# Attention and a mixture of experts on one core: early feed-forward blocks in fp16 for two resident experts, with weights loaded once and split in place

## The chip, the core and the metric

The kernel runs on one core of a Trainium2 chip. The metric is the device time of one execution in microseconds. A core has these engines: PE (TensorE, the matrix array, with PEld its weight loads), DVE (VectorE), ACT (ScalarE), POOL (GpSimd) and SP (SyncE, which issues most DMAs here). Each works through its own queue in order; semaphores tie them together.

## What is computed

Two layers follow each other. First an attention with a window of 128 keys and a bias that falls with distance, for 8 batches x 8 heads x 576 positions x 64 dimensions; then a mixture of 8 experts over the 4608 tokens of width 512, in which each token goes to its two best experts.

```python
# attention, per batch and head
scores = scale * q @ k.T + bias, where 0 <= row - column < 128, else -1e9
x = softmax(scores) @ v                                  # 4608 x 512 in all
# experts
noisy = x @ w_gate + log1p(exp(x @ w_noise)) * noise      # 4608 x 8
top2  = the two largest of noisy; g = softmax over the two
out[token] += g * (relu(x[token] @ w1[e]) @ w2[e])        # for both experts e; w1: 512 x 1024, w2: 1024 x 512
```

## The kernel before, in words

The program is written by a planner. Each piece of work is a small generator ("strand") that yields operations with an engine, an estimated duration and a rank; `Order.run` simulates the engines with these estimates and always issues the waiting operation of lowest rank. The result is a fixed order in each engine's queue. Where an operation may run on two engines (`either`, or an `Op` with two entries), the simulated engine that is free first takes it; constants such as `LATE` shift the rank for the second engine.

**Attention.** 32 pairs of heads (four to a batch) go through scores on PE (L455, L448), bias and row maximum on DVE (L473), exponentials on ACT (L480), transposes on PE (L492), their copies `pT` on ACT or DVE (L245, L249), and the product with the values on PE (L523). All in fp32. Per batch, `row_major` scales and stores x to DRAM (`xs`), and `gate` makes logits: a matmul (L655), a transpose, a product (L671) and a sum over the heads on DVE (L676).

**Routing.** When a batch's logits are there, `route(b)` picks the two best experts, counts ranks with matmuls, and builds each expert's list of tokens: a table of lines (`which_line`, one DVE instruction of 128x800, L759), a table of places (`which_place`, ten DVE instructions of 128x64, L765), and ten matmuls of the two (L770). The list is added to a table in DRAM by a GpSimd scatter (L843). Route b+1 waits for route b's scatter.

**Experts, early part.** After two batches (`CUTS = (2,)`), the first 256 list entries of experts 0 to 3 are computed while attention goes on: four blocks in fp32r. Each operand is split into a high and a low part, and three products (high x high, low x high, high x low) are summed. Weights come in eight chunks per expert, of w1 128x4x128 and of w2 128x512; a chunk is loaded to `raw1`/`raw2`, its high part is a copy on ACT or DVE, its low part a subtraction on GpSimd or DVE (L962). A block has 96 matmuls of 256 columns (L1086) and 48 of 512 (L1136).

**Experts, late part.** When all routes are sent (`second_wave`), the rest follows in fp16 with the same three products: experts 0 to 3 have blocks of 512 and 448 rows, experts 4 to 7 of 512, 384 and 320 rows. All weights are loaded a second time. fp16 needs a scale by a power of two: for expert 0 the weights' maximum is taken from the early chunks (L966), for the others from a load of their own (`mraw`, eight of 512 KB, L987, L988). Then `scaled_weight` makes the high part (ACT or DVE) and the low part (DVE, L1023). Gathered tokens get a scale each (`fit`: L1051, L440, L441, L1047 to L1049, and a copy), are transposed (L1066) and split (L1076). After the first product comes relu, with its high part on ACT or DVE (L1108, L1110) and its low part on DVE (L1125). The last block of an expert forms its second product transposed (L1141), and its rows are turned back (L1196). Results are scaled and added to the output by GpSimd scatters (L1215). A loop at the end treats experts with over 1216 tokens.

## Time and profile before

| | |
|---|---|
| time, median of 3 runs | 1222.68 us (1221.63 to 1223.39) |
| span of the profiled execution, first to last instruction | 1217.5 us |
| instructions | 20871 |
| last matmul of attention ends (L523) | 328.3 us |
| last list product (L770) | 393.3 us |
| last early block ends (L1136) | 413.8 us |
| first late matmul (L1086) | 428.6 us |
| last matmul | 1204.7 us |
| mean granted clock of PE | 0.988 |

The times in the lower part are counted from the span's start. A row of the profile's groups reads: line, engine, operation, written tile <- read tiles, shape, count | busy us, mean ns of one | idle us of the engine just ahead of them, and what ended it. A row of the timeline has start, duration, engine, line, operation and count. A row of the stretches has the stretch, its length, and for each engine the busy time and number of instructions, then the granted clock, the DMA share and GB/s. A row of one line's instructions has the shortest, median and longest in ns.

### The profile page before, as it was taken

What the parts mean: (1) busy time and instruction counts of PE and PEld (TensorE: products, weight loads), DVE (VectorE), ACT (ScalarE), POOL (GpSimd) and SP (SyncE); (2) the same over time, 40 slices, a digit from 0 to 9 for tenths busy, and PEclk for the clock granted to TensorE, in tenths of its full rate; (3) what the DMA queues carried; (4) which work ended last, traced back from release to release, by engine and by line L of the source; (5) the groups of instructions that cost most, each with busy time, mean ns of one, the idle gap of its engine ahead of it and who ended that gap; (6) DMA issues with size and microseconds to landing.
All of it is one profiled execution on the core that took longest, in us unless ns stands there. A gap on an engine that the chain in (4) does not pass through costs nothing.

```text
span 1217.5 us, 20871 instructions
## 1 busy us (share of the span) xinstructions
PE 1141.3 (94%) x7356; PEld 685.2 (56%) x7356; DVE 765.7 (63%) x2493; ACT 542.2 (45%) x1362; POOL 292.5 (24%) x332
## 2 busy tenths in 40 slices
PE   6998999989987699999999999999999999999995
PEld 4666676667766444545545545445745664575552
DVE  7799887888888893574565646643763473363310
ACT  8777766667633542433424424422632341253211
POOL 5000111241245502033123213302223320322211
PEclk9999999999999889999999999999999999999998
DMA  8896544453266773564655636613763282342221
GB/s 287 303 306 224 162 146 148 142 163 107 67 186 162 191 250 71 181 190 73 192 144 110 186 112 157 187 57 61 206 176 61 54 271 58 62 113 45 35 26 23
DMA packets 133626, 173.35 MB, mean 142 GB/s; under 512 B 25489, under 2 KB 85137, under 8 KB 133521
## 3 DMA queue, kind: packets, MB, share of 16 engines
q1 hardware_dynamic: 115600, 131.68, 34.0%
q0 software_dynamic: 17920, 40.33, 17.5%
q8 instruction: 59, 0.97, 0.3%
q14 instruction: 47, 0.38, 0.1%
HBM read 130.57 MB, written 41.40 MB: 141 GB/s over the span
## 4 chain that ended last, share of the span: by engine, by line
PE 73%; DVE 15%; DMA 7%; issue 2%; ACT 2%; POOL 1%; SPq 0%; another core or an unknown queue 0%; POOLq 0%; DVEq 0%; ACTq 0%
PE bank L1086 26%; PE bank L1136 19%; PE bank L1141 8%; PE bank L523 5%; PE bank L492 4%; PE bank L455 4%; DMA mraw<-in_w_dram 4%; DVE wam L988 3%; PE bank L1066 2%; DMA raw<-in_w_dram 2%; DVE p L473 1%; PE bank L632 1%; DVE hot L765 1%; DMA xg<-xs_dram,ix 1%; PE bank L655 1%
## 5 line engine op out<-in xcount | busy, mean ns | idle before, releaser
L1125 DVE SCALAR_TENSOR_TENSOR bhl<-bank,bhh 128x512 f16<-128x512 f32 (+3 forms) x160 | 97.3, 608 | 300.5 <-ACT bhh L1108 300.4
L1215 POOL DMA_INDIRECT out_dram<-yo,ix x72 | 113.7, 1580 | 560.6 <-ACT yo L245 452.9
L1108 ACT ACTIVATE bhh<-bank 128x512 f16<-128x512 f32 (+3 forms) x150 | 80.4, 536 | 354.5 <-PE bank L1086 353.5
L1086 PE MATMUL bank<-bxh,w1hb 128*128 128x512 f16 (+3 forms) x640 | 223.0, 348 | 0.7 <-ACT bxh L245 0.7
L1086 PE MATMUL bank<-bxl,w1hb 128*128 128x512 f16 (+3 forms) x640 | 222.9, 348 | 0.1
L1086 PE MATMUL bank<-bxh,w1lb 128*128 128x512 f16 (+3 forms) x640 | 222.9, 348 | 0.0
L1086 PEld LDWEIGHTS <-w1hb 128*128 128x128 f16 x1280 | 124.8, 98 | 107.8 <-issue 4.3
L1136 PE MATMUL bank<-w2hb,bhl 128*128 128x512 f16 (+1 forms) x376 | 142.6, 379 | 4.4 <-DVE bhl L1125 4.4
L1136 PE MATMUL bank<-w2hb,bhh 128*128 128x512 f16 (+1 forms) x376 | 142.8, 380 | 0.5 <-ACT bhh L1108 0.5
L1136 PE MATMUL bank<-w2lb,bhh 128*128 128x512 f16 (+1 forms) x376 | 142.5, 379 | 0.0
L480 ACT ACTIVATE p<-p,nm 128x256 f32<-128x256 f32 (+2 forms) x288 | 133.7, 469 | 13.3 <-DVE nm L473 13.2
L1136 PEld LDWEIGHTS <-bhh 128*128 128x128 f16 (+1 forms) x752 | 72.0, 98 | 78.2 <-issue 4.6
L473 DVE CUSTOM_DVE_ANT_0 p<-bank,bias 128x256 f32<-128x256 f32 (+2 forms) x288 | 95.5, 380 | 15.2 <-PE bank L455 11.8
L1086 PEld LDWEIGHTS <-w1lb 128*128 128x128 f16 x640 | 62.8, 98 | 55.9 <-issue 1.2
L523 PE MATMUL bank<-pT,vraw 128*64 128x128 f32 (+3 forms) x896 | 81.0, 303 | 5.3 <-ACT p L480 2.7
L492 PE MATMUL bank<-ident,p 128*128 128x128 f32 x512 | 83.2, 285 | 1.8 <-ACT p L480 0.5
L1034 POOL DMA_INDIRECT xg<-xs_dram,ix x72 | 71.5, 993 | 50.5 <-ACT bxh L245 25.4
L988 DVE TENSOR_REDUCE wam<-mraw 128x1 f32<-128x1024 f32 x56 | 67.4, 1210 | 18.1 <-DMA mraw<-in_w_dram 18.1
L455 PE MATMUL bank<-qk 64*128 64x256 f32 (+1 forms) x512 | 69.9, 383 | 8.8 <-DMA qk<-in_qk_dram 4.7
L962 POOL TENSOR_TENSOR w1la<-raw,w1ha 128x512 fp32r<-128x512 f32 x28 | 38.3, 1367 | 156.2 <-ACT w1ha L245 94.6
L1141 PE MATMUL bank<-bhl,w2hb 128*128 128x448 f16 (+1 forms) x224 | 73.8, 330 | 0.0
L1141 PE MATMUL bank<-bhh,w2hb 128*128 128x448 f16 (+1 forms) x224 | 73.8, 330 | 0.0
(219 smaller groups left out, 2007.6 us busy)
## 6 DMA issues: line engine op xcount, KB each, us to landing
raw<-in_w_dram SPq DMA_DIRECT2D x192, 256.0 KB, 3.6
mraw<-in_w_dram SPq DMA_DIRECT2D x56, 512.0 KB, 6.7
qk<-in_qk_dram SPq DMA_DIRECT2D x32, 608.0 KB, 4.3
out_dram<-xg SPq DMA_DIRECT2D x10, 1024.0 KB, 8.3
vraw<-in_v_dram SPq DMA_DIRECT2D x16, 512.0 KB, 4.5
xs_dram<-x SPq DMA_DIRECT2D x32, 256.0 KB, 4.0
vraw<-in_v_dram SPq DMA_DIRECT2D x16, 128.0 KB, 4.9
xg<-xs_dram,ix POOLq DMA_INDIRECT x72, 4.9
```

The lines of the kernel that those rows point to most:

```text
L455: nc.tensor.matmul(s[h][:, o:o + c], qk[half, i * 128:i * 128 + 128], qk[half, QW + k0:QW + k0 + c], start=True, stop=True)
L473: nc.vector.tensor_tensor_reduce(out=p[:, z, h, 0:c], in0=s[h][:, o:o + c], in1=bv, scale=-0.125, scalar=3.0e38, op0=OP.add, op1=OP.min, a ...
L480: nc.scalar.activation(pv, pv, AF.Exp, bias=nm[:, z, h:h + 1], scale=-1.0, accum_out=den[:, z, 2 * g + h:2 * g + h + 1])
L492: nc.tensor.transpose(t[:, z], p[:, h, a:a + 128], ident)
L523: nc.tensor.matmul(o[half, o0:o0 + c], t[p0:128, kb, hh:hh + D], w, start=m == 0, stop=m == len(lst) - 1)
L988: yield dve(1.13, rank, lambda: nc.vector.tensor_reduce(o, t, axis=AX.X, op=OP.max, apply_absolute_value=True))
L1086: nc.tensor.matmul(t[:, 0:blk.n], wp[:, c], x[:, c, 0:blk.n], start=c == 0 and z == 0, stop=c == 3 and z == 2)
L1108: nc.scalar.activation(o, i, AF.Relu)
L1125: yield dve(0.07 + c * 0.00104, rank - MIDDLE, lambda: nc.vector.scalar_tensor_tensor(hl[:, 0:c], t[:, 0:c], 0.0, high, op0=OP.max, op1=OP ...
L1136: nc.tensor.matmul(blk.y[j][0:r], h[:, cs], wp, start=f == 0 and m == 0, stop=f == 7 and m == 2)
L1141: nc.tensor.matmul(blk.y[c][:, 0:blk.n], wp[:, c * 128:c * 128 + 128], h[:, 0:blk.n], start=f == 0 and m == 0, stop=f == 7 and m == 2)
L1215: ins = nc.gpsimd.indirect_dma_start(out=out, out_offset=bass.IndirectOffsetOnAxis(ap=blk.ix[0:r, j:j + 1], axis=0), in_=t[0:r], in_offset ...
```

## The change

- **Early blocks.** `CUTS = (2, 4, 6)`: after two, four and six batches, 256 more list entries of experts 0 and 1 alone are computed: six blocks, in fp16 with `fit`, in the sequence (0,0), (0,1), (1,0), (1,1), (0,2), (1,2) of expert and cut. The late blocks of experts 0 and 1 shrink to one of 448 rows; experts 2 to 7 have 512, 384 and 320.
- **Weights.** Each weight is loaded once. A held tile of 128x1024 fp32 takes a chunk of w1 and w2; there are 16, and 8 more from the second wave on, with 2 spares. The maximum is taken from the loaded chunk (the loads of `mraw` go). The split writes the four fp16 parts into a spare tile; when both halves are split, the raw tile is the next spare. The tiles of experts 0 and 1 stay until their late block is done; an expert's tiles go back when its last block has used them.
- **GpSimd.** The low parts of experts 0 and 1 may run on GpSimd as two instructions (scale, subtract). For all batches but the last, the head sums of the logits run on GpSimd in three additions, and the two tables are made in narrow compares (four for each of five row groups) on GpSimd or DVE.
- Durations, ranks and thresholds of the planner have new numbers, so all orders move. Of this table:

```diff
-CUTS = (2,)
-FIRST = (256,)
-NF = 4
+CUTS = (2, 4, 6)
+EARLY, STEP = 2, 256
-BLOCKS = (((256, 512), (768, 448)), ((0, 512), (512, 384), (896, 320)))
+BLOCKS = (((768, 448),), ((0, 512), (512, 384), (896, 320)))
+HELD, MORE = 16, 8
+SEQUENCE = ((0, 0), (0, 1), (1, 0), (1, 1), (0, 2), (1, 2))
```

The logits and the tables:

```diff
-        yield dve(0.36 if nz == 1 else 0.5, rank, lambda: nc.vector.tensor_reduce(
-            lgs[b % 2][0:rows, i:i + nz], lt[0:rows, 0:nz].rearrange("p z h e -> p z e h"), axis=AX.X, op=OP.add))
+            G.tensor_add(lv[:, :, 0:4], lv[:, :, 0:4], lv[:, :, 4:8])
+            G.tensor_add(lv[:, :, 0:2], lv[:, :, 0:2], lv[:, :, 2:4])
+            G.tensor_add(lgs[b % 2][0:rows, i:i + nz], lv[:, :, 0], lv[:, :, 1])
...
+        def tables(eng, i):
+            for k in range(2):
+                eng.tensor_scalar(hot[0][:, 2 * i + k], steps_, ef[:, i, k:k + 1], None, op0=OP.is_equal)
+            which_place(eng, i)
...
-        yield dve(0.98, rank, which_line)
-        for i in range(NQ):
-            yield dve(0.28, rank, lambda: which_place(i))
+        if b == B - 1:
+            yield dve(0.98, rank, which_line)
+            for i in range(NQ):
+                yield dve(0.41, rank, lambda: which_place(nc.vector, i))
+        else:
+            for i in range(NQ):
+                yield Op((("POOL", 1.36, rank), ("DVE", 0.86, rank + LATE[10])), lambda g: tables(engine[g], i))
```

The weights:

```diff
+    def weight(e, f, z, t, src, rank):
         yield from move(2.6e5, rank, lambda: nc.sync.dma_start(t, src))
-        yield either(0.52, 0.34, rank, LATE[5], lambda g: copy(g, hi, t))
-        yield Op((("POOL", 1.23, rank), ("DVE", 0.6, rank + WEIGHTS_LATE)),
-                 lambda g: engine[g].tensor_sub(lo, t, hi.bitcast(F32)))
+        yield dve(0.6, rank + (BIG if e >= EARLY else 0), lambda: nc.vector.tensor_reduce(
+            wam[:, e % 2, z, f:f + 1], t, axis=AX.XY if z == 0 else AX.X, op=OP.max, apply_absolute_value=True))
+        mark(seen[e])
+
+    def parts_of_weights(e):
+        yield seen[e]
+        yield from powers_of_weights(e, early_rank(e, 0) + (BIG if e >= EARLY else 0))
+        for f in range(8):
+            rank = early_rank(e, f) + (PARTS if e >= EARLY else 0)
+            t = yield (spares, rank)
+            chunks[e, f] = [Event(), Event(), halves_of(t), t]
...
+                spawn(split(e, f, z, raws(held_[e, f])[z], halves_of(t)[2 * z:2 * z + 2], rank, both))
+            spawn(turn_over(both, held_[e, f]))
...
+    def split(e, f, z, t, parts, rank, both):
...
+        yield either(0.52, 0.6, rank, LATE[5], lambda g: copy(g, hi, t, scale=sc))
+        def low(g):
+            if g == "POOL":
+                nc.gpsimd.tensor_scalar(t, t, sc, None, op0=OP.mult)
+                nc.gpsimd.tensor_sub(lo, t, hi)
+            else:
+                nc.vector.scalar_tensor_tensor(lo, t, sc, hi, op0=OP.mult, op1=OP.subtract)
+        if e < EARLY:
+            yield Op((("POOL", 2.3, rank), ("DVE", 0.66, rank + WEIGHTS_LATE)), low)
+        else:
+            yield dve(0.66, rank, lambda: low("DVE"))
```

Order on DVE and GpSimd, where the tables of the third batch are made (`ef` holds the line and `d` the place of each row, `hot` the two tables). DVE before:

```order
L759 TENSOR_TENSOR hot_167<-ef,steps 128x800
L473 ISA p_86,nm_90<-bank_66,bias_127 128x192
L473 ISA nm_90 128x1
L765 TENSOR_SCALAR hot_168<-steps,d,numbers 128x64 x2
L249 COPY xu_94<-bank_70 128x256
L765 TENSOR_SCALAR hot_168<-steps,d,numbers 128x64 x2
```

GpSimd now, ahead of the scatter of the same list:

```order
L777 TENSOR_SCALAR hot_179<-steps,ef 128x80 x2
L783 TENSOR_SCALAR hot_180<-steps,d,numbers 128x64 x2
L777 TENSOR_SCALAR hot_179<-steps,ef 128x80 x2
L783 TENSOR_SCALAR hot_180<-steps,d,numbers 128x64 x2
L864 MEMSET pad 1x1
L865 DMA slots_dram<-listed,line_of_158 704x64
L682 TENSOR_TENSOR lt_111<-lt_111 128x2x64
```

The tables have left DVE's queue, where attention's maxima stood between them, and stand one behind the other in GpSimd's, with the next batch's logit sums behind the scatter.

Order on PE, where the last early block meets the first late one (`ahh`, `ahl` are the early blocks' parts behind relu, `bxh`, `bxl` the late blocks' tokens). Before:

```order
L1136 MATMUL bank_70<-w2ha_180,ahh_212 128x512
L1136 MATMUL bank_70<-w2la_181,ahh_212 128x512
L1136 MATMUL bank_70<-w2ha_180,ahl_214 128x512
L1066 MATMUL bank_69<-ident,xg_121 128x128 x4
L1066 MATMUL bank_69<-ident,xg_122 128x128 x4
L1066 MATMUL bank_69<-ident,xg_123 128x128 x4
L1066 MATMUL bank_69<-ident,xg_124 128x128 x4
L1086 LDWEIGHTS w1hb_4531
L1086 MATMUL bank_66<-bxh_4521,w1hb_4531 128x512
```

Now:

```order
L1145 MATMUL bank_73<-held_128,ahh_211 128x512
L1145 LDWEIGHTS ahl_214
L1145 MATMUL bank_73<-held_128,ahl_214 128x512
L1097 LDWEIGHTS spare_131
L1097 MATMUL bank_66<-bxh_4602,spare_131 128x448
L1097 LDWEIGHTS spare_131
L1097 MATMUL bank_66<-bxl_4604,spare_131 128x448
```

The transposes of the late tokens no longer stand between the two parts; they stand ahead, among early matmuls. In PE's order the last matmul of attention now has 4.31 of six early blocks behind it (2.38 of four before), and the last list product three of six (about 0.7 of four before).

More of the change, by code (lines that the diff above doesn't have):

```diff
@@ L276, in attention_moe @@
     zero = zeros[:, 0:DM]
-    scratch = [z.rearrange("p a b -> p (a b)") for z in raw1.free]
+    scratch = spares.free
     relc, m1 = scratch[0][:, 0:256], scratch[0][:, 256:512]
@@ L361, in columns @@
             nc.vector.tensor_copy(line_of[0], first_line)
-            nc.vector.tensor_scalar(least[:, 0], iota8, float(NF), float(FIRST[0]), op0=OP.is_lt, op1=OP.mult)
+            for z in range(len(CUTS)):
+                nc.vector.tensor_scalar(least[:, z], iota8, float(EARLY), float(STEP * (z + 1)), op0=OP.is_lt, op1=OP.mult)
         yield pool(0.4, 2, small)
@@ L900, in block_rings @@
                 "hh": ring(pool_, hn, [128, c], dt, name + "hh"), "hl": ring(pool_, hn, [128, c], dt, name + "hl")}
-    wsets = [Ring([weight_set(keep, F32R, f"a{z}") for z in range(5)]), Ring([])]
     wam = keep.tile([128, 2, 2, 8], F32, name="wam")
@@ L907, in attention_moe @@
     back = keep.tile([128, E], F32, name="back")
-    seen = {(e, f): Event(2) for e in range(EARLY) for f in range(8)}
+    seen = [Event(16) for _ in range(E)]
     sized = [Event() for _ in range(E)]
@@ L911, in attention_moe @@
     yor = ring(keep, 2, [128, DM], F32, "yo")
-    rings1 = block_rings(keep, FIRST[0], F32R, "a", 2)
+    rings1 = block_rings(keep, STEP, F16, "a", 3)
     ixr, ytr = Ring([]), Ring([])
-    first = [Block(e, 0, FIRST[0], CUTS[0] * S, rings1) for e in range(NF)]
+    first = [Block(e, STEP * z, STEP, CUTS[z] * S, rings1) for e, z in SEQUENCE]
+    for blk, (_, z) in zip(first, SEQUENCE):
+        blk.cut = z
     second, lists2 = [], []
-    fitr = Ring([])
+    fitr = ring(keep, 4, [128, 3], F32, "fit")
     chunks = {}
@@ L1009, in powers_of_weights @@
         mark(sized[e])
-    def all_powers():
-        for e in range(EARLY):
-            for f in range(8):
-                yield seen[e, f]
-            yield from powers_of_weights(e, ranks1[8 * e + 7] + SIZES[0])
-    def scaled_weight(t, r, hi, lo, ev, rank, src, e, z, f):
-        yield from move(2.6e5, rank, lambda: nc.sync.dma_start(t, src))
-        yield sized[e]
-        sc = wsc[:, e, z:z + 1].bitcast(F32)
-        yield either(0.52, 0.6, rank, LATE[5], lambda g: copy(g, hi, t, scale=sc))
-        yield dve(0.6, rank, lambda: nc.vector.scalar_tensor_tensor(lo, t, sc, hi, op0=OP.mult, op1=OP.subtract))
-        put(r, t)
-        mark(ev)
     def tokens(blk, rank):
@@ L1057, in turn_tokens @@
         yield order.now + 2.3
-        if blk in second:
-            yield from fit(blk, j, r, xg, rank)
+        yield from fit(blk, j, r, xg, rank)
         a = yield (tb, rank)
@@ L1100, in ups @@
                 yield (own, rank)
-            us = 3 * (blk.n / 2400 + (0.005 if p else 0.016))
-            for c in range(4):
-                end = yield pe(us, rank, lambda: mm1(blk, t, ev[2], (c,)), False)
+            us = 3 * (blk.n / 2400 + 0.005)
+            for cc in ((0, 1, 2, 3),) if blk.cut is not None else ((0,), (1,), (2,), (3,)):
+                end = yield pe(us * len(cc) + (0.1 if blk.cut is not None else 0.0), rank,
+                               lambda: mm1(blk, t, ev[2], cc), False)
             spawn(middle(blk, f, t, rank, end))
@@ L1123, in middle @@
             e, hh[:, 0:c], t[:, 0:c]))
[L1124 removed]
         yield dve(0.07 + c * 0.00104, rank - MIDDLE, lambda: nc.vector.scalar_tensor_tensor(
[L1126 removed]
+            hl[:, 0:c], t[:, 0:c], 0.0, hh[:, 0:c], op0=OP.max, op1=OP.subtract))
         put(hbr, t)
@@ L1175, in after @@
         if w:
-            if p == 0 and blk.e < EARLY:
-                yield seen[blk.e, f]
-            put(wsets[p], w)
+            put(held, w)
     def flipped(blk, c, rank, end):
@@ L1255, in second_wave @@
         rings2 = block_rings(more, 512, F16, "b", 3)
-        for z in range(10):
-            put(wsets[1], weight_set(more, F16, f"b{z}"))
+        for z in range(HELD, HELD + MORE):
+            put(held, more.tile([128, 2 * DM], F32, name=f"held{z}"))
         for z in range(2, 3):
@@ L1263, in second_wave @@
         for z in range(4):
-            put(fitr, more.tile([128, 3], F32, name=f"fit{z}"))
-        for z in range(4):
             put(ixr, more.tile([128, 4], I32, name=f"ix{z}"))
-        spawn(size_of_weights(ring(more, 3, [128, 1024], F32, "mraw")))
         t = yield (tb, 0)
         put(yb, t)
-        second.extend(Block(e, s0, c, NPAD, rings2) for e in range(E) for s0, c in BLOCKS[e >= NF])
+        second.extend(Block(e, s0, c, NPAD, rings2) for e in range(E) for s0, c in BLOCKS[e >= EARLY])
         for blk, after_ in zip(second, second[1:] + [None]):
```

215 lines of the change are left out of this document (100 added, 115 removed).

## The prediction

> **What bounds the kernel now.** I read the page's head first, then the busy time of each engine in three stretches: up to the last matmul of attention, from there to the first matmul of the late feed-forward blocks, and the late blocks themselves.
>
> ```profile
> span 1217.5 us, 20871 instructions
> PE 1141.3 (94%) x7356; PEld 685.2 (56%) x7356; DVE 765.7 (63%) x2493; ACT 542.2 (45%) x1362; POOL 292.5 (24%) x332
> ...
> core 0: us, PE busy (x) PEld busy (x) DVE busy (x) ACT busy (x) POOL busy (x), PEclk, DMA share, GB/s
> 0.00:328.10 328.10, 303.89 (x2724) 218.42 (x2724) 273.74 (x1245) 230.74 (x815) 59.94 (x75) 1.00 0.59 189
> 328.10:428.60 100.50, 75.92 (x523) 61.86 (x522) 87.65 (x260) 40.53 (x85) 52.03 (x49) 0.92 0.66 177
> 428.60:1204.70 776.10, 761.45 (x4113) 404.92 (x4112) 404.31 (x991) 270.23 (x462) 176.26 (x204) 1.00 0.47 120
> ```
>
> The late stretch is PE alone: 761 of 776 us busy, every other engine near half. There, only fewer columns save time. In the first two stretches DVE is busy for 83% and 87%, and PE's busy time overstates it, since a matmul's record outlives the start of the next. The starts show the true rate:
>
> ```profile
> 371.06 0.28 PE L1086 MATMUL bank<-axh,w1ha 128*128 128x256 f32 x1
> 371.18 0.28 PE L1086 MATMUL bank<-axl,w1ha 128*128 128x256 f32 x1
> ...
> 373.57 0.40 PE L1136 MATMUL bank<-w2ha,ahh 128*128 128x512 f32 x1
> 373.80 0.40 PE L1136 MATMUL bank<-w2la,ahh 128*128 128x512 f32 x1
> ...
> 1000.08 0.38 PE L1136 MATMUL bank<-w2hb,bhh 128*128 128x512 f16 x1
> 1000.29 0.38 PE L1136 MATMUL bank<-w2lb,bhh 128*128 128x512 f16 x1
> ```
>
> An early fp32r matmul of 256 columns starts 0.12 us after the one ahead, one of 512 columns 0.23 us; an fp16 one of 512 takes 0.215 us. An early block has 96 matmuls of 256 columns and 48 of 512, so 11.5 + 11.0 = 22.5 us of PE in fp32r.
>
> **Term 1, the late blocks: about -46 us.** Their first matmuls are these (the L523 row is the end of attention):
>
> ```profile
> 327.69 0.60 PE L523 MATMUL bank<-pT,vraw 128*64 128x64 f32 x8
> ...
> 428.61 0.58 PE L1086 MATMUL bank<-bxh,w1hb 128*128 128x512 f16 x1 [0.69 <-ACT bxh L245]
> ...
> 473.17 0.35 PE L1086 MATMUL bank<-bxh,w1hb 128*128 128x448 f16 x1
> ...
> 512.32 0.38 PE L1086 MATMUL bank<-bxh,w1hb 128*128 128x512 f16 x1
> ...
> 770.39 0.38 PE L1086 MATMUL bank<-bxh,w1hb 128*128 128x512 f16 x1
> ...
> 1204.31 0.38 PE L1136 MATMUL bank<-w2hb,bhl 128*64 128x512 f16 x1
> ```
>
> A 448-row block takes 512.32 - 473.17 = 39.1 us. The four experts of 1216 late rows take (1204.7 - 770.4) / 4 = 108.6 us each, the four of 960 rows (770.4 - 428.6) / 4 = 85.4 us. After the change two experts have one late block of 448 rows and six have 1216 rows: 2 x 39.1 + 6 x 108.6 = 729.8 us against 776.1, so 46.3 us less. Counting matmuls alone, 512 rows fewer are 192 starts of 0.215 us, 41.3 us; I take 46, since transposes and waits leave with their rows, and keep 41 as the other end.
>
> In this stretch the weight work must stay hidden. Each expert loses 16 fresh loads or 8 size loads, and its 16 maxima of 512 columns replace 8 of 1024:
>
> ```profile
> L988 DVE TENSOR_REDUCE wam<-mraw 128x1 f32<-128x1024 f32 x56 | 67.4, 1210 | 18.1 <-DMA mraw<-in_w_dram 18.1
> L966 DVE TENSOR_REDUCE wam<-w1ha 128x1 f32<-128x512 f32 x8 | 5.4, 676 | 0.0
> L1023 DVE SCALAR_TENSOR_TENSOR w1lb<-raw,wsc,w1hb 128x512 f16<-128x512 f32 x64 | 47.8, 746 | 0.7
> ...
> raw<-in_w_dram SPq DMA_DIRECT2D x192, 256.0 KB, 3.6
> ```
>
> 16 x 0.676 = 10.8 us stands against 8 x 1.21 = 9.7 per expert, and the low parts (0.746 each) fall from 128 to 96. DVE stays at half of this stretch, and a new expert's eight held tiles are free at least one whole expert ahead, so I cost it at nothing; if the cover fails, it is one wait of some 4 us (a load lands 3.6 us after its issue) for each of six experts, 24 us at worst.
>
> **Term 2, the end of attention: 0, within 12 us.** DVE sets its pace, so I added up DVE's rows up to the last score in the order before and after.
>
> ```profile
> L249 DVE COPY pT<-bank 128x512 f32<-128x512 f32 (+1 forms) x59 | 33.5, 571 | 8.4 <-PE bank L492 7.4 <-ACT pT L245 0.6 <-ACT p L480 0.2
> L676 DVE TENSOR_REDUCE lg<-lt 128x32 f32<-128x256 f32 (+1 forms) x24 | 12.1, 505 | 0.3
> L765 DVE TENSOR_SCALAR hot<-steps,d,numbers 128x64 f16<-128x64 f16 x80 | 26.5, 379 | 0.0
> L759 DVE TENSOR_TENSOR hot<-ef,steps 128x800 f16<-128x800 f32 x8 | 9.9, 1237 | 0.0
> L1051 DVE TENSOR_REDUCE fit<-xg 128x1 f32<-128x512 f32 x72 | 48.6, 677 | 5.7 <-DMA xg<-xs_dram,ix 5.7
> ```
>
> Off DVE go 18 logit sums (9 us), five wide compares (6 us), 26 of 50 narrow ones (10 us) and 24 copies of pT that the order now gives to ACT (14 us): 39 us. On it come 16 more maxima (11 us), 14 low parts (10 us), 8 high parts (4 us), five x copies (3 us) and the scaling of six gathered tiles at some 1.4 us (8 us, with 3 us of copies): 39 us. The gain on the tables is spent on the split of the resident weights. ACT has room for its copies (231 of 328 us busy). The ends of this term: -12 us if the additions fit into DVE's idle sixth (55 us) and a third of what leaves is won, +12 if as much of them comes on top.
>
> Loads move too. Of 64 early weight loads 16 stood at the front of SP's queue, the rest came in between the batches; now all 32 stand there, 4.2 MB more, and most of the zeroing of the output (ten stores of 1 MB) stands behind them.
>
> ```profile
> GB/s 287 303 306 224 162 146 148 142 163 107 67 186 162 191 250 71 181 190 73 192 144 110 186 112 157 187 57 61 206 176 61 54 271 58 62 113 45 35 26 23
> ```
>
> The first 90 us run at about 300 GB/s, so that is 14 us of transfers, covered by the first pairs' inputs, which stay ahead of them, and by the zeroing that gives way; without that cover attention would start its fifth pair up to 14 us late, inside the +12.
>
> GpSimd takes 108 narrow compares, 63 logit sums and 22 low parts of two instructions. Its own rows bound them:
>
> ```profile
> L349 POOL IOTA steps<- 128x80 f16 x1 | 0.2, 209 | 0.0
> L962 POOL TENSOR_TENSOR w1la<-raw,w1ha 128x512 fp32r<-128x512 f32 x28 | 38.3, 1367 | 156.2 <-ACT w1ha L245 94.6 <-DVE w1ha L249 27.0 <-PE bank L1086 15.9
> ```
>
> Below by 0.21 us (80 columns written), above by 1.37 (two inputs of 512). By columns, 80 and 64 lie near the first row; I take 0.3 us, so 20 in a route are 6 us, as long as DVE needs now (1.24 + 10 x 0.38 = 5.0). At 1.37 us they would be 27 us.
>
> One lock bears on this. Here are the spreads of the two table groups (min/median/max):
>
> ```profile
> L765 DVE TENSOR_SCALAR hot<-steps,d,numbers x80: 207/291/2870, 86.1 to 392.8; 128x64 f16<-128x64 f16 x80
> L759 DVE TENSOR_TENSOR hot<-ef,steps x8: 981/986/2003, 85.2 to 385.5; 128x800 f16<-128x800 f32 x8
> ```
>
> The narrow one has a median of 0.29 us and a worst of 2.87, the wide one 0.99 and 2.00: something holds them up. The Trainium skill, page "SBUF — State Buffer", section "Who interferes with whom", says that DVE and GpSimd share one pair of ports as an exclusive lock, for DVE instructions in a two-port mode or with two SBUF inputs. By that rule the tables stop being victims (80 x 0.09 + 8 x 0.25 = 9 us), but the 28 low parts, high parts and scalings that DVE gains ahead of attention's end can each lose up to one GpSimd instruction of 1.37 us: between -9 and +29 us of DVE. My sum stays at 0 with the ends above.
>
> **Term 3, from attention's end to the first late matmul: about +14 us.** Before, it is 100.5 us and holds
>
> ```profile
> L1086 PE MATMUL bank<-axh,w1ha 128*128 128x256 f32 x76 | 23.0, 303 | 0.0
> ...
> L1136 PE MATMUL bank<-w2ha,ahl 128*128 128x512 f32 x38 | 16.7, 438 | 10.5 <-DVE ahl L1125 9.6 <-DVE fit L440 0.9
> ...
> 372.61 0.23 ACT L708 ACTIVATE u<-lg 128x40 f32<-128x40 f32 x1
> ...
> 393.27 0.85 PE L770 MATMUL bank<-hot,hot 128*80 128x64 f16 x10
> ...
> 413.43 0.39 PE L1136 MATMUL bank<-w2ha,ahl 128*128 128x512 f32 x1
> ```
>
> three times 76 and three times 38 matmuls, 2.38 blocks or 53.6 us of PE, and by my count of small transposes and gate products 12 us more: a third of the stretch is waiting, on DVE and on the last batch's route, whose list is built at 393.3. The early blocks end at 413.8; then PE has nothing but token transposes until 428.6. In the new order 4.31 of six blocks follow attention. An fp16 matmul of 256 columns is not in this trace; half of 0.215 gives 0.108 us, the fp32r row 0.12. By the first a block is 96 x 0.108 + 48 x 0.215 = 20.7 us, by the second 21.8; I take 20.7, as 512 columns already run at the faster rate. So 89 us of blocks and 12 of the rest are 101 us without a wait. 1.31 blocks lie ahead of the last list, three behind it. If that list comes 49 us after attention (65 now; two routes wait for one another there, and the order places the sixth list 2.7 pairs of heads sooner), then 49 + 62 + 4 = 115 us; if it comes as late as now, 131; with no wait, 101. The tail hides the gather and scaling of the late tokens, 35 us now from the list to the first late matmul. I take 115, so +14 us; ends 0 and +31.
>
> **Sum.** 1217.5 - 46 + 0 + 14 = 1185.5 us of span. The 12.8 us behind the last matmul (the output scatters) stay. The median of the runs, 1222.7, is 5.2 us over the profiled span; on that scale 1190.7, so 1190 us. DMA traffic falls by 64 weight loads of 256 KB and 56 of 512 KB, which frees nothing PE waits for.
>
> **Rivals.** *Attention gains too*: the tables leave DVE, its other additions fall in holes, and the list comes early: -12 in term 2 and +2 in term 3 give 1166. For it: 83% busy DVE; against: the added rows equal the removed ones. 15%. *The routes stay in line*: the list comes 65 us after attention, or DVE's 28 two-input and scaling instructions wait for GpSimd, at half of 1.37 us each 19 us: 1205 to 1217. For it: 9.6 us of PE waits for DVE's `ahl` already, and the worst of 2.87 us above. 15%. (The second of these is what the lock of the page "SBUF — State Buffer" in the Trainium skill would do here.) *GpSimd's small instructions have a price that hardly falls with size* (slower): GpSimd runs in order, so the scatter of a batch's list, the next batch's logit sums and the gathers stand behind its 20 compares, and PE's in-order list product waits for them. A route takes 20 to 30 us now (372.6 to 393.9 for the last) and a batch some 41; from about 0.8 us a compare the routes outlast the batches, and at 1.37 each of seven falls some 6 us behind, 42 us at the end, with three early blocks still to come behind the last list: with the 8 us that the product and scatter add, 115 becomes about 165, so 1240. Against: the 0.21 us row. 10%. *The parts cancel* within 0.2% (1220 to 1225): 4%. The Trainium skill, page "GPSIMD Engine Reference", section "3.1 Elementwise — side-by-side cycle accounting", gives 2.6 cycles at 1.2 GHz an element for two inputs: 1.11 us for 512 columns, where the row has 1.37. By it a compare of 80 columns would be, as an estimate, 0.17 us and the 0.26 that the row has over it, far under 0.8; it speaks against the slower rival.
>
> **How the numbers follow.** My forecast, 1176 to 1204 us, has 56%; the others 15, 15, 10 and 4. Faster by over 0.2% (about what runs of this kernel can tell from no change): 86%. Within: 4%. Slower: 10%. The range of 8 in 10 takes in the forecast, most of the first two rivals, and leaves out the slow one: 1163 to 1217.
>
> **What would show it.** First late matmul 443 us after the start, and from there to the last matmul 730 us: that is term 1, the surest. The early fp16 matmuls start 0.108 us apart. Attention's last matmul at 328, within 12. The last list 49 us behind it. Compares on GpSimd near 0.3 us. I would be wrong if these reach 0.8, if PE's waits for the list's tables exceed 20 us, or if the late blocks wait for held weights.

## The result, and the profile after

| | before | after | forecast |
|---|---|---|---|
| time, median of 4 runs each | 1222.16 us (1220.69 to 1223.39) | 1177.24 us (1173.26 to 1179.60) | 1190 (1163 to 1217) |
| ratio, 95% interval | | 0.9621 (0.9596 to 0.9646) | |
| span of the profiled execution | 1217.5 | 1176.5 | 1185.5 |
| attention's last matmul starts | 328.1 | 335.0 | 328 |
| last list product starts, behind it by | 65 | 32 | 49 |
| first late matmul | 428.6 | 446.6 | 443 |
| late blocks | 776.1 | 717.2 | 730 |

The change makes the kernel 3.8% faster, some 45 us where 33 were forecast. The page's head and the busy time of each engine in the same three stretches:

```profile
span 1176.5 us, 21215 instructions
PE 1125.6 (96%) x7588; PEld 682.6 (58%) x7588; DVE 703.2 (60%) x2479; ACT 529.9 (45%) x1364; POOL 365.7 (31%) x495
...
core 0: us, PE busy (x) PEld busy (x) DVE busy (x) ACT busy (x) POOL busy (x), PEclk, DMA share, GB/s
0.00:335.00 335.00, 311.18 (x2817) 216.44 (x2819) 275.92 (x1285) 243.62 (x856) 155.12 (x248) 0.97 0.59 185
335.00:446.60 111.60, 102.56 (x739) 68.38 (x740) 85.88 (x306) 40.39 (x83) 37.81 (x48) 0.98 0.44 100
446.60:1163.80 717.20, 711.83 (x4036) 397.79 (x4034) 341.39 (x890) 245.25 (x425) 168.53 (x195) 1.00 0.36 75
```

DVE does in the first stretch what it did before (276 us against 274), as the sums of the forecast said, but the stretch is 7 us longer. GpSimd goes from 60 to 155 us there. The late stretch is PE alone still. The borders, from the timeline of PE (the two L1097 rows are the first late block and the first block of expert 2):

```profile
334.63 0.60 PE L525 MATMUL bank<-pT,vraw 128*64 128x64 f32 x8
...
367.31 0.54 PE L788 MATMUL bank<-hot,hot 128*80 128x64 f16 x10
...
425.72 0.38 PE L1097 MATMUL bank<-axh,held 128*128 128x256 f16 x2
425.94 0.27 PE L1097 MATMUL bank<-axl,held 128*128 128x256 f16 x1
426.05 0.38 PE L1097 MATMUL bank<-axh,held 128*128 128x256 f16 x2
...
446.56 0.35 PE L1097 MATMUL bank<-bxh,spare 128*128 128x448 f16 x1
...
525.80 0.38 PE L1097 MATMUL bank<-bxh,held 128*128 128x512 f16 x1
...
1163.41 0.38 PE L1145 MATMUL bank<-held,bhl 128*64 128x512 f16 x1
```

Three early matmuls of 256 columns take 426.05 - 425.72 = 0.33 us, so they start 0.11 us apart, as taken. The groups that answer to those of before:

```profile
L987 DVE TENSOR_REDUCE wam<-held 128x1 f32<-128x512 f32 x120 | 79.4, 678 | 10.8 <-DMA held<-in_w_dram 10.4
L1018 DVE SCALAR_TENSOR_TENSOR held<-held,wsc,held 128x512 f16<-128x512 f32 x89 | 64.1, 761 | 0.0
L250 DVE COPY pT<-bank 128x512 f32<-128x512 f32 (+1 forms) x34 | 19.9, 590 | 3.2 <-PE bank L494 3.0
...
L1015 POOL TENSOR_SCALAR held<-held,wsc 128x512 f32<-128x512 f32 x22 | 36.4, 1656 | 47.6 <-ACT spare L246 44.8 <-ACT held L246 2.8
L783 POOL TENSOR_SCALAR hot<-steps,d,numbers 128x64 f16<-128x64 f16 x54 | 30.7, 574 | 0.0
L777 POOL TENSOR_SCALAR hot<-steps,ef 128x80 f16<-128x80 f16 x54 | 25.4, 476 | 33.2 <-DVE ef L754 21.3 <-PE bank L668 7.4 <-PE bank L494 4.5
L1016 POOL TENSOR_TENSOR held<-held,held 128x512 f16<-128x512 f32 x19 | 23.4, 1234 | 1.6
```

A narrow compare takes 0.48 or 0.57 us on GpSimd, not the 0.3 of the forecast, and not the 0.8 from which it saw trouble. A low part takes two instructions, 1.66 and 1.23 us in the mean. How the compares stand in a route, on GpSimd's timeline:

```profile
99.01 0.96 POOL L777 TENSOR_SCALAR hot<-steps,ef 128x80 f16<-128x80 f16 x2 [1.24 <-DVE ef L754]
99.96 1.14 POOL L783 TENSOR_SCALAR hot<-steps,d,numbers 128x64 f16<-128x64 f16 x2
...
109.05 1.13 POOL L783 TENSOR_SCALAR hot<-steps,d,numbers 128x64 f16<-128x64 f16 x2
110.12 0.09 POOL L864 MEMSET pad<- 1x1 f32 x1
111.07 1.67 POOL L865 DMA_INDIRECT slots_dram<-listed,line_of  x1 [0.86 <-DVE wex L442]
```

Eleven microseconds in a row, a few sums of the next batch among them, where DVE needed five. What PE's list product waits for directly is little (its own rows, from all eight routes):

```profile
  POOL hot L783: 3.4, 5
  issue: 2.0, 3
  POOL hot L777: 0.9, 3
```

More hangs on these waits than their own length. PE's granted clock is 0.97 in the first stretch, where it was 1.00 before. It stands near 0.50 in three places, 17 us in all:

```profile
109.90:116.80 6.90, 6.57 (x37) 4.12 (x37) 4.32 (x24) 3.96 (x14) 3.22 (x4) 0.51 0.47 115
157.70:164.60 6.90, 5.26 (x28) 3.49 (x28) 5.67 (x25) 3.19 (x12) 6.51 (x5) 0.51 0.50 161
195.30:198.70 3.40, 3.40 (x20) 2.39 (x17) 0.35 (x2) 2.34 (x9) 1.53 (x1) 0.50 0.13 6
```

Two of them begin just behind a wait of the list product for GpSimd's tables, the third behind a wait of 1.82 us for DVE's row maxima (L475, at 156.93):

```profile
109.67 0.19 PE L788 MATMUL bank<-hot,hot 128*80 128x64 f16 x1 [1.09 <-POOL hot L783]
...
193.78 0.19 PE L788 MATMUL bank<-hot,hot 128*80 128x64 f16 x1 [1.29 <-POOL hot L783]
```

At half the clock, 17 us hold as much of PE's work as some 9 us at the full one (an estimate from these rows), and attention ends 7 us later than before. No run changes the clock alone, so it is not shown that the waits lowered it, nor what that cost.

### The profile page after: what moved, and what is told of

The parts are those of the page before. It is cut to its first block, busy times and chain, and to the rows that moved or that the text cites. A ratio compares the mean times of both kernels' runs of the same rounds, so it can differ in the third digit from the quotient of the medians.

```text
span 1176.5 us, 21215 instructions
## 1 busy us (share of the span) xinstructions
PE 1125.6 (96%) x7588; PEld 682.6 (58%) x7588; DVE 703.2 (60%) x2479; ACT 529.9 (45%) x1364; POOL 365.7 (31%) x495
## 4 chain that ended last, share of the span: by engine, by line
PE 74%; DVE 10%; DMA 6%; POOL 4%; issue 3%; ACT 1%; another core or an unknown queue 1%; SPq 0%; POOLq 0%; DVEq 0%; ACTq 0%
PE bank L1097 30%; PE bank L1145 22%; PE bank L1150 7%; PE bank L525 3%; PE bank L494 3%; PE bank L457 3%; PE bank L1083 3%; DMA held<-in_w_dram 2%; DVE p L475 2%; DMA xg<-xs_dram,ix 1%; POOL hot L783 1%; DMA xg<-xs_dram,cl 1%; DVE held L1018 1%; PE bank L634 1%; DVE wam L987 1%
## 5 line engine op out<-in xcount | busy, mean ns | idle before, releaser
L1097 PE MATMUL bank<-bxh,held 128*128 128x512 f16 (+3 forms) x1168 | 321.5, 336 | 0.0
L1097 PEld LDWEIGHTS <-held 128*128 128x128 f16 x2256 | 220.0, 98 | 139.5 <-issue 2.9
L1134 DVE SCALAR_TENSOR_TENSOR bhl<-bank,bhh 128x384 f16<-128x384 f32 (+3 forms) x160 | 93.3, 583 | 291.0 <-ACT bhh L1118 284.7
L1118 ACT ACTIVATE bhh<-bank 128x384 f16<-128x384 f32 (+3 forms) x150 | 76.8, 512 | 338.9 <-PE bank L1097 336.6
L1145 PE MATMUL bank<-held,bhh 128*128 128x512 f16 (+1 forms) x664 | 197.8, 379 | 0.5 <-ACT bhh L1118 0.5
L1097 PE MATMUL bank<-bxl,held 128*128 128x384 f16 (+3 forms) x584 | 196.4, 336 | 0.0
L1145 PE MATMUL bank<-held,bhl 128*128 128x512 f16 x332 | 125.8, 379 | 0.0
L475 DVE CUSTOM_DVE_ANT_0 p<-bank,bias 128x256 f32<-128x256 f32 (+2 forms) x288 | 95.3, 379 | 12.3 <-PE bank L457 9.6
L1150 PE MATMUL bank<-bhh,held 128*128 128x320 f16 (+1 forms) x400 | 89.9, 314 | 0.0
L987 DVE TENSOR_REDUCE wam<-held 128x1 f32<-128x512 f32 x120 | 79.4, 678 | 10.8 <-DMA held<-in_w_dram 10.4
L525 PE MATMUL bank<-pT,vraw 128*64 128x256 f32 (+3 forms) x896 | 81.9, 303 | 1.4 <-ACT pT L246 0.6
L1150 PEld LDWEIGHTS <-held 128*128 128x128 f16 x600 | 58.6, 98 | 31.8 <-issue 1.5
```

The lines of the kernel that those rows point to most:

```text
L475: nc.vector.tensor_tensor_reduce(out=p[:, z, h, 0:c], in0=s[h][:, o:o + c], in1=bv, scale=-0.125, scalar=3.0e38, op0=OP.add, op1=OP.min, a ...
L525: nc.tensor.matmul(o[half, o0:o0 + c], t[p0:128, kb, hh:hh + D], w, start=m == 0, stop=m == len(lst) - 1)
L987: yield dve(0.6, rank + (BIG if e >= EARLY else 0), lambda: nc.vector.tensor_reduce(wam[:, e % 2, z, f:f + 1], t, axis=AX.XY if z == 0 els ...
L1097: nc.tensor.matmul(t[:, 0:blk.n], wp[:, c], x[:, c, 0:blk.n], start=c == 0 and z == 0, stop=c == 3 and z == 2)
L1134: yield dve(0.07 + c * 0.00104, rank - MIDDLE, lambda: nc.vector.scalar_tensor_tensor(hl[:, 0:c], t[:, 0:c], 0.0, hh[:, 0:c], op0=OP.max, ...
L1145: nc.tensor.matmul(blk.y[j][0:r], h[:, cs], wp, start=f == 0 and m == 0, stop=f == 7 and m == 2)
```

## Experiments: GpSimd or DVE

The forecast took DVE for the engine that sets attention's pace. Then moving tables to GpSimd should help, and moving them back hurt. The first two runs ask that. *Tables on DVE* makes all routes as the last one is made:

```diff
-        if b == B - 1:
+        if True:
             yield dve(0.98, rank, which_line)
```

> All eight routes make their tables on DVE, as before the change (one wide and ten narrow instructions); the rest is the changed kernel (1177 us). Theory A (the sum of the prediction: what the tables free on DVE is spent again on the weights' split, and PE's waits, not DVE's load, set the pace): DVE gains about 7 x 5.0 - 13 = 22 us ahead of attention's end, a part of it falls into idle time; 1177 to 1190. Rival B (moving the tables to GpSimd is what pays): 1197 or more, attention's end at 355 or later in place of 335.

Ratio 0.9612 (0.9589 to 0.9635), median 1171.15 us: not told apart from the changed kernel by ratio, and below what either theory gave. In the profiled execution the span is 1167.2 us and attention ends at 328, 7 us sooner; PE's clock is near half there for 3.5 us of attention (131.2 to 134.7) in place of 17. This execution is the fastest of its four, that of the changed kernel the second slowest of four, so the spans differ by more than the ratios do. Nothing was lost by giving DVE the tables.

*Nothing on GpSimd* moves the logit sums and the low parts of experts 0 and 1 to DVE too:

```diff
-        if b == B - 1:
+        if True:
             yield dve(0.36 if nz == 1 else 0.5, rank, lambda: nc.vector.tensor_reduce(
...
-        if b == B - 1:
+        if True:
             yield dve(0.98, rank, which_line)
...
-        if e < EARLY:
+        if False:
             yield Op((("POOL", 2.3, rank), ("DVE", 0.66, rank + WEIGHTS_LATE)), low)
```

> Tables, logit sums and low parts all on DVE, nothing of the three on GpSimd; early fp16 blocks and weights loaded once stay. DVE gets about 22 + 9 + 16 = 47 us more ahead of attention's end. Theory A: a third to a half of it shows, 1190 to 1205, still faster than before (1222). Rival B (the offload pays for the whole gain): 1217 or more.

Ratio 0.9537 (0.9515 to 0.9559), median 1162.15 us: about 10 us faster than the changed kernel by ratio, where theory A had 1190 or more, and attention ends 16 us sooner. Its first stretch:

```profile
0.00:318.70 318.70, 302.60 (x2795) 211.89 (x2795) 284.74 (x1322) 250.61 (x872) 23.39 (x48) 1.00 0.61 196
```

DVE is busy for 285 of 319 us, 89%. A busy share of 83% with idle holes is no proof that an engine sets the pace: here it carries 9 us more work in 16 us less time. PE's granted clock is 1.00 throughout this stretch, so a part of the 16 us is clock.

*Each compare twice* on GpSimd tests the slower rival, whose point was 0.8 us a compare:

```diff
+            for _ in range(2 if eng is nc.gpsimd else 1):
                 for k in range(2):
                     eng.tensor_scalar(hot[0][:, 2 * i + k], steps_, ef[:, i, k:k + 1], None, op0=OP.is_equal)
                 which_place(eng, i)
```

> Each compare on GpSimd is made twice, so a pair of one 80-column and one 64-column compare costs about 2.1 us there in place of 1.04, 10 us more for a route; the plan is the same. The prediction's slower rival set the point of trouble at 0.8 us a compare. Theory A: routes still fit in a batch, so most of the 10 us is hidden but PE's list product waits some us in each of seven routes: +5 to +20 us, 1182 to 1197. Rival C (the routes' chain decides at once): +40 us and more, 1217 or later. If nothing waits for GpSimd: within 3 us of 1177.

Ratio 1.0141 (1.0115 to 1.0166), median 1236.68 us: slower than the kernel before, as rival C had it and not theory A. Attention's end moves from 335 to 388 us, and PE's waits have a new head:

```profile
PE bank L789 <- POOL hot L784: 51.0, 25, 5.8
```

The 54 + 54 compares added are 25.4 + 30.7 = 56 us, and the time grows by 59, about as much, while in the run with the tables on DVE 56 us taken off GpSimd bring 9 us of span at most. The 59 are not GpSimd's time alone: PE's granted clock is 0.92 up to attention's end (0.97 in the changed kernel), and the missing 8% of 388 us are 31 us at full clock, an estimate of what PE lost by it if it had no slack. At an effective 1.04 us a compare, the time comes near the 1240 that the rival had put on 1.37: its mechanism is real and dearer than it was priced, for a value the kernel doesn't have.

Were the planner's durations to blame, since it took 1.36 us for four compares (measured: 2.09) and 2.3 for a low part (2.75, near the median; the mean is 2.9)?

```diff
-                yield Op((("POOL", 1.36, rank), ("DVE", 0.86, rank + LATE[10])), lambda g: tables(engine[g], i))
+                yield Op((("POOL", 2.09, rank), ("DVE", 1.07, rank + LATE[10])), lambda g: tables(engine[g], i))
...
-            yield Op((("POOL", 2.3, rank), ("DVE", 0.66, rank + WEIGHTS_LATE)), low)
+            yield Op((("POOL", 2.75, rank), ("DVE", 0.66, rank + WEIGHTS_LATE)), low)
```

> The planner is told the durations that the profile shows: 2.09 us for four compares on GpSimd (it had 1.36), 1.07 on DVE (0.86), 2.75 us for a low part on GpSimd (2.3); every order moves a little. Theory A (PE waits in the first stretch come from orders made with too short times): 2 to 10 us less, 1167 to 1175. Rival: the orders are as good as each other, 1174 to 1181; or worse, since the other numbers were set with the old durations, 1181 to 1190.

Ratio 0.9625 (0.9598 to 0.9652): no difference that can be told. The median, 1171.96 us, lies in theory A's range, but the kernel before was faster in that call too (1219.59 us, against 1222.16 with the result). Nearly every edit here makes the planner place the operations anew; this run, which changes only the order and with it the choice of engine, is the one measure of what that does by itself.

Which of the moves costs? *Only the sums on GpSimd*:

```diff
-        if b == B - 1:
+        if True:
             yield dve(0.98, rank, which_line)
...
-        if e < EARLY:
+        if False:
             yield Op((("POOL", 2.3, rank), ("DVE", 0.66, rank + WEIGHTS_LATE)), low)
```

> The changed kernel with the tables and the low parts of resident weights on DVE; the sums of the logits stay on GpSimd. With the tables alone on DVE the time was 6 us under the changed kernel, with the sums and low parts on DVE too 15 us. Theory A: the low parts on GpSimd cost the other 9 us, by the port that DVE and GpSimd share (two instructions, 2.7 us each, 64 of them); then this kernel lies within 2 us of the one with nothing on GpSimd, 1161 to 1165 us. Theory B: the sums cost them, since they stand in GpSimd's in-order queue behind scatters and gathers: 1168 to 1172 us.

Ratio 0.9509 (0.9480 to 0.9538), median 1161.64 us: theory A. The sums are harmless; the low parts are what costs, 0.9612 - 0.9509 or some 13 us (9.5 by the medians) against the run with only the tables moved back. Attention ends at 320, 8 us sooner than there. The clock is not the reason: it is near half for 3.5 us of attention there and for 3.4 us here.

Why do they cost? I summed over all DVE instructions up to 345 us what each took beyond the median of its own line and shape. The kernel before loses 11 us so, the changed one 10, the one with the tables on DVE 13, the one with the sums alone 1.8, the one with nothing on GpSimd 0.2. (Coarser groups make the first three 1 to 3 us larger and leave the last two.) In the changed kernel and in the one before, over 80% of it lies on instructions that overlap a low part on GpSimd (L1015 and L1016, before L962). Most of the victims are small instructions of the route and of the softmax. One line of them (shortest, median, longest ns), in the changed kernel and in the one with nothing on GpSimd:

```profile
L606 DVE TENSOR_SCALAR den<-den x24: 155/164/1150, 38.1 to 336.0; 128x16 f32<-128x16 f32 x16, 64x8 f32<-64x8 f32 x8
```

```profile
L606 DVE TENSOR_SCALAR den<-den x24: 109/164/170, 38.1 to 320.2; 128x16 f32<-128x16 f32 x16, 64x8 f32<-64x8 f32 x8
```

If that is so, the kernel before has the same trouble. *The kernel before with all early low parts on DVE*:

```diff
-        yield Op((("POOL", 1.23, rank), ("DVE", 0.6, rank + WEIGHTS_LATE)),
-                 lambda g: engine[g].tensor_sub(lo, t, hi.bitcast(F32)))
+        yield dve(0.6, rank, lambda: nc.vector.tensor_sub(lo, t, hi.bitcast(F32)))
```

> The kernel before with the low parts of its early weights all on DVE (52 of 64 ran on GpSimd at 1.28 us; on DVE one takes 0.68, so DVE gains 35 us up to 404 us, where it was 83 to 87 per cent busy). Theory A: GpSimd's work with two inputs holds DVE up (DVE lost 11.9 us against its own medians), and DVE has room for 35 us: the time is 0 to 10 us less. Theory B: DVE sets the pace up to the last list, as I took it for the prediction: 10 to 30 us more.

Ratio 0.9882 (0.9844 to 0.9920), median 1207.40 us: some 14 us faster, more than theory A's 10, though DVE takes 52 more low parts, 35 us by their rows. DVE's busy time in the whole execution stays where it was (765.7 before), since held-up instructions became shorter and the planner placed other work anew:

```profile
PE 1137.8 (94%) x7356; PEld 684.8 (57%) x7356; DVE 766.2 (63%) x2539; ACT 542.6 (45%) x1368; POOL 227.2 (19%) x280
```

Attention ends at 321 instead of 328, and the last early matmul starts at 386 instead of 413. The narrow table compares, whose worst took 2870 ns before, now have

```profile
L765 DVE TENSOR_SCALAR hot<-steps,d,numbers x80: 207/293/297, 85.2 to 381.2; 128x64 f16<-128x64 f16 x80
```

A low part on GpSimd also takes time in GpSimd's queue, ahead of sums, gathers and scatters. *Idle fills* puts such time back, without low parts, into the run with only the sums on GpSimd:

```diff
+    def idle_fills(rank):
+        def fills():
+            for _ in range(5):
+                nc.gpsimd.memset(blank, 0.0)
+        yield pool(2.75, rank, fills)
...
+        if e < EARLY and 2 * f + z < 11:
+            spawn(idle_fills(rank))
```

> The changed kernel with tables and low parts on DVE, as the run that leaves only the sums on GpSimd (1161.6 us), and in the places of 22 low parts five fills of a tile that nobody reads on GpSimd, 22 x some 2.7 us, for which nobody waits. The changed kernel gave GpSimd 22 low parts. Theory A: what the low parts cost is DVE waiting for GpSimd's instructions that read two tiles (DVE lost 10 to 16 us against its own medians in the kernels that have them, 1.8 us in the one that has none); fills of GpSimd's time alone cost little: 1160 to 1166 us, DVE loses under 4 us. Theory B: the time that they take in GpSimd's in-order queue, ahead of sums, gathers and scatters, is the price: 1167 to 1173 us. If DVE loses 10 us or more beside the fills too, the fills hold DVE up as the low parts did, and the two can't be told apart by this run.

```profile
L1013 POOL MEMSET blank<- 128x512 f32 x110 | 58.3, 530 | 5.8
```

Ratio 0.9543 (0.9511 to 0.9574), median 1168.96 us. The median lies in theory B's bounds, but the kernel before also ran 3 us longer in that call than in the one of the sums alone; by ratio the fills cost 0.0034 or 4 us, with both intervals overlapping, and the low parts 13. DVE loses 7 to 8 us here, so the result falls between what was written down. Occupancy alone is not the price, since 58 us of it would then have cost about as much as the 60 us of low parts in the run with the tables on DVE. Whether the rest is the held-up DVE alone, or also a low part that takes 2.9 us instead of 0.76 and so gives its tile back later, stays open. None of PE's waits in the changed kernel ends on a low part (its rows for POOL name `hot` and `pad` alone), but the order itself may hold PE's work back until the weights are due; DVE and ACT wait 4.6 us for the second instruction of low parts (L1016).

The lost time agrees with the Trainium skill, page "SBUF — State Buffer", section "Who interferes with whom", in more than direction. It says that a DVE instruction with two SBUF inputs contends with a GpSimd instruction that reads SBUF, and not with one that only writes it, while copies, casts and `tensor_scalar` in a two-port mode contend with GpSimd without that limit. Beside the low parts, which read, the losers were of all these kinds (a `TENSOR_TENSOR` on `l` lost 0.58 us in the changed kernel); beside the fills, which only write, 17 `TENSOR_SCALAR`, one `COPY` and one `CAST` lost time, and none of the 39 `TENSOR_TENSOR` that overlap a fill.

## Experiments: the late blocks

They came out 13 us shorter than forecast. In the kernel before, I compared each late PE start with the median distance of its kind: 751.3 us at the medians and 24.4 us over them; after, 707.0 and 9.8. So waits went that the forecast had left in. Some 3 us of them lie in the first 25 us of the stretch, where PE's granted clock is 0.92 before and 1.00 after. The change replaced the loads and maxima of `mraw`. *The kernel before without them* (scales of all experts from expert 0's maxima):

```diff
-            for z, src in enumerate((w1, w2)):
-                for q in range(4):
-                    t = yield (rg, rank)
-                    spawn(largest(rg, t, rank, wam[:, e % 2, z, q:q + 1], dram(src, e * DM * F + q * 1024, [[4096, 128], [1, 1024]]),
-                                  done))
-            yield done
...
-        n_ = 8 if e < EARLY else 4
-        yield dve(0.1, rank, lambda: V.tensor_reduce(wmx, wam[:, e % 2, :, 0:n_], axis=AX.X, op=OP.max))
+        n_ = 8
+        yield dve(0.1, rank, lambda: V.tensor_reduce(wmx, wam[:, 0, :, 0:n_], axis=AX.X, op=OP.max))
```

> The kernel before without the 56 size loads of 512 KB and their maxima: the scales of experts 1 to 7 come from expert 0's maxima; all else as before, also the second load of weights. Theory E (maxima on DVE held up PE in the late part): 8 to 15 us less, 1207 to 1214, with PE's waits in the late stretch falling from 24 us to some 10. Rival F: within 3 us of 1222.

Ratio 0.9865 (0.9827 to 0.9903), waits 11.5 us: 13 of the 14.6 us came from there. *The changed kernel with the maxima's DVE time added again* (one more maximum of 1024 columns for each chunk of experts 2 to 7, of data that is there):

```diff
+        if e >= EARLY and z == 1:
+            yield dve(1.13, rank + BIG, lambda: nc.vector.tensor_reduce(
+                spare_max, held_[e, f], axis=AX.X, op=OP.max, apply_absolute_value=True))
```

> The changed kernel with the maxima of before put back beside its own, for experts 2 to 7: for each chunk one more maximum over all 1024 columns of the held tile on DVE (1.2 us), into a tile that nobody reads; no load is added. DVE gets 58 us more, nearly all behind attention. Theory E (the late part lost 15 us of PE waits because DVE lost the maxima of 1024 columns): PE's waits there rise from 10 us by 5 to 15, total 1182 to 1192. Rival F (the waits went with the second loads, or with the start of the late part): within 3 us of 1177.

Ratio 0.9618 (0.9588 to 0.9648), waits 11.1 us: DVE's time alone is not the price. Then it is the loads' traffic, or DVE waiting for them. Two runs take the pair apart in the kernel before, first *loads only*, then *maxima only* (of tiles filled once), both with all scales from expert 0:

```diff
-        yield dve(1.13, rank, lambda: nc.vector.tensor_reduce(o, t, axis=AX.X, op=OP.max, apply_absolute_value=True))
...
```

```diff
-        yield from move(5.2e5, rank, lambda: nc.sync.dma_start(t, src))
...
```

> The kernel before with its 56 size loads of 512 KB, but without the 56 maxima that read them (the weights' scales are all taken from expert 0, so the computation differs there). The kernel before waits 24.4 us in its late blocks, and 11.5 without loads and maxima. Theory A: the price lies in DVE's in-order queue, where a maximum waits for its load and the scales of tokens wait behind it; with nobody reading the loads the late waits fall to 11 to 14 us and the time is 10 to 17 us under the kernel before. Theory B: the price is the traffic of the loads, which holds up gathers, weights or scatters; the waits stay at 21 to 25 us and the time within 5 us of the kernel before.

> The kernel before with the 56 maxima of 1024 columns kept, reading tiles that are filled once, and without the 56 loads (all scales from expert 0). Theory A (DVE waits for the loads): late waits of 11 to 15 us, time 9 to 17 us under the kernel before. Theory B (traffic): the same. Theory C (it is DVE's 1.2 us for each maximum that stands ahead of the tokens' scales): waits stay at 20 to 25 us, time within 5 us of the kernel before. Together with the run that keeps the loads alone, A, B and C have one answer each.

Ratios 0.9865 (0.9827 to 0.9902) and 0.9888 (0.9850 to 0.9926), late waits 9.9 and 7.4 us. Neither half alone can be told from none, both together cost 14 to 17 us: theory A. The 56 maxima, with the same 1.21 us of DVE each, no longer have idle time ahead of them:

```profile
L987 DVE TENSOR_REDUCE wam<-mraw 128x1 f32<-128x1024 f32 x56 | 64.7, 1207 | 0.0
```

How it costs stands in the chain of work of the kernel before, in the window of one expert:

```profile
524.46 1.14 DVE wam L988
525.61 6.70 DMA mraw<-in_w_dram
532.31 0.02 issue
532.33 1.22 DVE wam L988
533.55 0.60 DVE bhl L1125
...
534.28 0.02 issue
534.31 0.15 DVE fit L441
...
534.88 0.60 DVE bxl L1076
...
537.38 0.38 PE bank L435 x2
```

The 6.70 us are the load of 512 KB from issue to landing; DVE works through a part of them and then stands for 2.35 us at the maximum that needs it (its own row):

```profile
531.05 2.50 DVE L988 TENSOR_REDUCE wam<-mraw 128x1 f32<-128x1024 f32 x2 [2.35 <-DMA mraw<-in_w_dram]
```

Behind it in the same queue are the split of the current block (`bhl`) and the scales and splits of the next tokens, for which PE waits. PE's waits for these in all late blocks (in total, times, longest), in the kernel before:

```profile
PE bank L1066 <- DVE bxl L1076: 4.7, 5, 1.3
PE bank L1136 <- DVE bhl L1125: 4.4, 5, 1.2
```

and in the one with loads only:

```profile
PE bank L432 <- DVE bxl L1075: 2.2, 1, 2.2
...
PE bank L1135 <- DVE bhl L1124: 0.5, 1, 0.5
```

An expert of 1216 late rows takes 108.3 us in the kernel before (988.6 to 1096.9) and 105.1 in the one with loads only (980.7 to 1085.8).

## Experiment: the third early block

Are the blocks of the third cut worth their place? *Two cuts*: four early blocks, and experts 0 and 1 get late blocks of 384 and 320 rows.

```diff
-CUTS = (2, 4, 6)
-BLOCKS = (((768, 448),), ((0, 512), (512, 384), (896, 320)))
-SEQUENCE = ((0, 0), (0, 1), (1, 0), (1, 1), (0, 2), (1, 2))
+CUTS = (2, 4)
+BLOCKS = (((512, 384), (896, 320)), ((0, 512), (512, 384), (896, 320)))
+SEQUENCE = ((0, 0), (0, 1), (1, 0), (1, 1))
```

> Early blocks after two and four batches only: four fp16 blocks of 256 rows, as many rows as before the change; experts 0 and 1 have late blocks of 384 and 320 rows in place of one of 448. Late part longer by 2 x (63 - 39) = 48 us by the blocks' starts in the profile of before; the stretch behind attention shorter by up to two blocks, 41 us, as long as the last list and the gather behind it hide under the four blocks. Theory A (a row costs PE the same early or late; two blocks more only cover the wait for the last list): +5 to +12 us, 1182 to 1190. Rival D (early blocks run in PE time that is idle otherwise): +30 us or more, 1207 and later.

Ratio 0.9706 (0.9675 to 0.9737), median 1186.22 us: 10 us slower than the changed kernel, within theory A. Attention ends at 322 and the first late matmul comes at 402.5, 44 us sooner, but the late part is 50 us longer. So the same 512 rows lengthen the run by some 6 us less early than late in these two executions; where the rest of the 10 us lies is open. That the blocks of the third cut pay because they fill PE's wait for the last route was argued, and is not shown: from the list to the first late matmul it takes 38 us here and 79 with them.

## Why the forecast held, and where it was off

**Term 1, late blocks, -46 forecast, -59 measured: the rows were right, the waits were missed.** Experts 0 and 1 take 525.8 - 446.6 = 79.2 us (78.2 forecast from the 39.1 us block), the other six (1163.8 - 525.8) / 6 = 106.3 us each where 108.6 was carried over: 6 x 2.3 = 14 us, the whole difference. The step that failed is "DVE stays at half of this stretch ... I cost it at nothing". It weighed the maxima by their busy time alone (10.8 against 9.7 us) and put a risk on the new side; the row it quoted has 18.1 us of DVE idle time ended by the `mraw` load, and that wait stood in DVE's queue ahead of PE's next tokens. Removing the wait was a gain, and loads-only and maxima-only show that it was this wait and neither half of it.

**Term 2, end of attention, 0 forecast, +7 measured: inside its ends, but its reason fell.** The bookkeeping held (DVE 274 and 276 us, 25 copies of `pT` left DVE where 24 were counted). The premise "DVE sets its pace" did not: nothing on GpSimd gives DVE more work and ends attention 16 us sooner. In the profiled executions 7 us of that go with the tables (335 to 328) and 8 more with the low parts (328 to 320). The low parts' cost lay on the side of the lock that the forecast had given -9 to +29 us: they hold up DVE's small instructions. The tables were taken away from among the victims, but others took their place, so DVE loses about as much as before (10 and 11 us) instead of 9 us less. For the tables the trace names PE's waits for them on GpSimd (4.3 us) and the three stretches near half the clock, two of them behind such waits. The forecast took PE's clock as full and has no term for that; what share of the 7 us each has is not shown. That attention's end stayed inside the 12 us is in part luck.

**Term 3, from attention to the late blocks, +14 forecast, +11 measured: right in size, by two errors that cancel.** The list came 32 us behind attention, not 49, so "routes stay in line" fell. But from the list to the first late matmul it took 79 us, not 66: the three blocks were at their 21 us each (68 us at median distances, with the transposes of late tokens), and 11 us of waits came on top, of which PE's rows name

```profile
PE bank L1145 <- DVE ahl L1134: 6.2, 3, 4.2
...
PE bank L437 <- DVE ix L908: 1.4, 1, 1.4
```

**The sum.** -59 + 7 + 11 = -41 us of span, against -32. The median of the runs stands 0.7 us over the profiled span, where 5.2 was carried over from the kernel before; that is most of the rest of the 13 us between 1190 and 1177.

**The slower rival.** Its mechanism is real (compares made twice), and the steep part begins somewhere between 0.52 us, the mean of the two compares, and 1.04. The forecast chose 0.3 by columns, from a write of 80 columns at 0.21; that row was too low for a compare with a scalar of its own in each partition, and no run says why. The forecast's estimate from the Trainium skill, page "GPSIMD Engine Reference", section "3.1 Elementwise — side-by-side cycle accounting" (2.6 cycles an element for two inputs), was 0.17 and 0.26, together 0.43 us, close to the 0.48 measured here. A compare reads one tile, so that closeness may be luck.

**Best version.** The changed kernel with tables and low parts on DVE, 0.9509 of the time before: the early fp16 blocks and the weights that are loaded once carry the gain, and the part of the change that used GpSimd gives back about 14 us of it (0.9621 against 0.9509). Whether the sums stand on GpSimd or DVE can't be told apart (0.9509 and 0.9537).

## What to carry to other kernels

Read the third column of a group, the idle time ahead of it, before the busy time: an instruction that waits for a load in an in-order queue holds up everything queued behind it, so removing it can pay (14 to 17 us here) though the engine is half idle and its busy time alone costs nothing that can be told. Before moving work off an engine that looks full, move some onto it and time that: at a share of 83%, DVE took 9 us more in one kernel and 52 low parts more in the other, and both became faster. Work moved to GpSimd can cost in three ways, by its own duration where someone waits for it, by its place in that queue, and by the time for which it holds up small DVE instructions; the last is seen by comparing the longest instruction of a line with its median. Look at PE's granted clock beside its waits: a short wait can stand ahead of a stretch at half the clock that is several times as long.

## What was not expected of the hardware

A GpSimd compare of 64 or 80 fp16 columns took 0.57 and 0.47 us against 0.30 and 0.24 on DVE (medians of the same lines). GpSimd's scaling of 512 fp32 columns by a scalar of each partition took 1.66 us in the mean, more than its subtraction of two inputs (1.23). Behind a PE wait of 1.1 us the granted clock stood at 0.51 for 6.9 us. And fills that read nothing still held DVE up, by 0.1 to 0.5 us at a time, but only its copies, casts and `tensor_scalar`s.
